# An output projection whose contraction drops from 4 row tiles to 3.5, with two heads sent into spare rows by DMA and the work after it moved in the issue order

## The chip, the cores and the metric

One core of a Trainium2 chip runs the whole kernel. Times are device microseconds (us). The trace is of one profiled execution of the same program. Engines: PE is the matrix engine (PEld its weight loads), ACT, DVE and POOL are the scalar, vector and general engines, and SP is the engine whose queue issues nearly all the DMAs of this kernel.

## The reference

Two transformer layers over x of shape [1, 2048, 448]: attention with 16 query heads of 28 columns and a single key and value head, then a gated feed-forward block. Both layers use the same weights.

```
q = (x @ wq) in 16 heads of 28;  k = x @ wk;  v = x @ wv
p = softmax(q . k / sqrt(28));   o = p @ v, the 16 heads side by side: 448 columns
attention(x) = o @ wo                               # the output projection
ffn(x)       = (silu(x @ w_gate) * (x @ w_up)) @ w_down
x = x + attention(layernorm(x));  x = x + ffn(layernorm(x))      # twice
```

## The kernel before, in words

The order of instructions on each engine is the order in which the code is written (manual scheduling): every engine works down its own list and waits on semaphores. What the change touches lies in the attention stage, `Attention.scores` (L600), run once in each layer.

**Work items.** The 2048 queries are four chunks c of 512 (NC = 4), the 16 heads four groups g of four (NG = 4). An item i = 4c + g is one group of heads on one chunk; i runs from 0 to 15. For each item the 16 key tiles kt are gone through (NT = 16), so the loop counter is n = 16 i + kt, and two key tiles make a double step d = n // 2. All three-term products use a value split into a rounded part and its remainder ("h" and "l" tiles).

**One step** (`step`, L630): 12 matmuls (L639), four heads at once in four strips of 32 rows of PE, write the scores of three heads into a `three` of three PSUM banks and of the fourth into a single bank (`one`, bank 6 or 7). ACT takes the exponentials: L651 (single bank) and L652 (`three`) in even steps, L646 (`three`) and L649 in odd ones, where DVE first copies the single bank out (L648, `raw`). After both steps of a double step, `pv` (L673) multiplies the probabilities of the double step before by the values (L680, 16 matmuls) into a single bank, and DVE adds that to the item's accumulator (L690, or L687 for the first).

**The end of an item** (`post` and `rest`, L694 to L722). Row 28 of each strip of 32 holds a head's denominators. They go by DMA to a small tile `rs` (L701). Three double steps later, at kt = 4 of the following item, DVE takes bounds and the reciprocal (L707 to L709), two DMAs spread the result through DRAM over the rows (`rd` L711, `o<-rd` L712), and POOL multiplies (L719) and splits into `onh`, `onl` (`split`, L139 and L140).

**The output projection** (`outproj`, L617). When the four items of chunk 0, 1 or 2 are done, the projection of that chunk is issued in `between` (L655) at kt = 10 of item 4c + 4: 4 row tiles of queries, each 4 groups x 3 terms = 12 matmuls of 128 rows x 448 columns, into two banks of `three`, then `one`, then the other single bank; each tile is followed by a DVE addition into the residual `xres` (L626). In a group's 128 rows only 4 x 28 carry heads; the rows of `wo` in between are set to zero (`load_wo`, L609, in items 2 and 3 at kt = 8). Chunk 3 is projected behind the loop.

**The layer norm of the finished chunk** is spread over key tiles by a table `later` (L726 to L738), from n = 16 (4c + 5) on: four statistics (DVE L240, L241), at offset 4 `scale` (POOL L246, L247: the reciprocal standard deviation `rstd`), from offset 5 on `apply` (DVE L255, reads `rstd`) and `turn` (DVE L260) by turns, then a DMA.

**Also on POOL:** at kt = 0 the split of the next item's queries (`parts`, L445), and at kt = 8 of items 11, 12 and 13 `weights` (L754): loads of the first feed-forward weights and 12 casts on POOL.

Of the kernel before, what the change touches and what calls it, by code (L numbers as in the profile page):

```python
# [9 lines left out]
F32R = mybir.dt.float32r  # L10
AF = mybir.ActivationFunctionType
ALU = mybir.AluOpType
# [3 lines left out]
P = 128  # L16
S = 2048
D = 448
H = 16
DH = 28  # L20
F = 1792
EPS = 1e-5
NT = S // P
NC = S // 512
NG = H // 4
# [27 lines left out]
def forward(  # L53
# [14 lines left out]
    nc = tc.nc  # L68
# [7 lines left out]
    wos = wo.rearrange("(g j d) n -> j d g n", g=NG, j=4)  # L76
# [46 lines left out]
    def dma(dst, src):  # L123
        nc.sync.dma_start(dst.bitcast(F32), src.bitcast(F32))
# [13 lines left out]
    def split(hi, lo, raw):  # L138
        nc.gpsimd.tensor_scalar(hi, raw, 1.0, 0.0, ALU.mult, ALU.add)  # L139
        nc.gpsimd.tensor_tensor(lo, raw, hi, ALU.subtract)  # L140

    xres = pers.tile([P, NT, D], F32, name="xres")
# [27 lines left out]
    def weights(fc):  # L170
        tiles, steps = parted(*loaded(fc))
        for f in steps:
            f()
        return tiles
# [178 lines left out]
    def side_by_side(lower, upper):  # L353

        assert len(lower) == len(upper)
        for two in zip(lower, upper):
            for po, (a, b), start, stop in two:
                nc.tensor.matmul(po, a, b, start=start, stop=stop, skip_group_check=True)  # L358
# [10 lines left out]
    class Attention:  # L369
# [230 lines left out]
        def scores(self, ff):  # L600
            next(switch)
            with tc.tile_pool(name=f"at{self.layer}", bufs=1, reuse_waits="tile") as wp:
                woh = wp.tile([P, NG, D], F32R, name="woh")
                wol = wp.tile([P, NG, D], F32R, name="wol")
                on, accs, pts = {}, {}, {}
                todo, due = [], {}
                single = lambda d: banks[6 + d % 2]

                def load_wo(z):  # L609
                    r = wpool.tile([P, 4, 2, P], F32, name="wr").rearrange("p (z k) b n -> p z (k b n)", z=2)  # L610
                    nc.gpsimd.memset(r, 0.0)
                    for j in range(4):
                        nc.sync.dma_start(r[32 * j : 32 * j + DH, :, 0:D], wos[j][:, 2 * z : 2 * z + 2, :])
                    zs = slice(2 * z, 2 * z + 2)
                    split(woh[:, zs, :], wol[:, zs, :], r[:, :, 0:D])

                def outproj(c, t, po, gs=range(NG)):  # L617
                    oh, ol = on[c]
                    ts_ = slice(P * t, P * t + P)
                    for g in gs:  # L620
                        for z, (a, b) in enumerate(((oh, woh), (oh, wol), (ol, woh))):
                            nc.tensor.matmul(  # L622
                                po[:, 0:D], a[:, g, ts_], b[:, g, :], start=(g + z == 0), stop=(g == NG - 1 and z == 2)
                            )
                    if gs[-1] == NG - 1:
                        return lambda: nc.vector.tensor_tensor(  # L626
                            xres[:, 4 * c + t, :], po[:, 0:D], xres[:, 4 * c + t, :], ALU.add
                        )
# [26 lines left out]
                def between(d):  # L655

                    i, kt = divmod(2 * d, NT)
                    free, one = threes[0], single(d + 1)
                    if full:
                        self.lent = free[:, 0, :]  # L660
                        if 6 <= kt < 14:
                            self.advance(min(NM // 4, NM * (i + 2) - self.done))
                        if kt == 14 and i + 1 < len(GR):
                            self.places[i + 1](free[:, 1, :])
                    if not todo or kt != 10:
                        return
                    c = todo.pop()
                    for f in [outproj(c, t, free[:, t, :]) for t in range(2)]:
                        f()
                    outproj(c, 2, one)()  # L670
                    outproj(c, 3, single(d))()

                def pv(d):  # L673

# [19 lines left out]
                def post(i):  # L694

                    c, g = GR[i]
                    out2 = accs.pop(i)
                    oraw, rb = out2[:, 0, :], out2[:, 1, :]
                    rs = wp.tile([P, 16], F32, name="rs", bufs=2)
                    for j in range(4):  # L700
                        nc.sync.dma_start(rs[32 * j : 32 * j + 32, :], oraw[32 * j + DH : 32 * j + DH + 1, :])  # L701

                    def rest():
                        if fine is not None:
                            under = wp.tile([P, 16], F32, name="under", bufs=2)
                            for bound, op in ((LIMIT, ALU.is_lt), (1.0 / LIMIT, ALU.is_gt)):
                                nc.vector.tensor_scalar(under, rs, bound, None, op)  # L707
                                nc.vector.tensor_tensor(fine, fine, under, ALU.mult)
                        nc.vector.reciprocal(rs, rs)  # L709
                        rd = dram.tile([4, 512], F32, name="rd", bufs=2)  # L710
                        nc.sync.dma_start(rd.rearrange("j (p n) -> (j p) n", n=16), rs)  # L711
                        nc.sync.dma_start(rb, rd[:, None, :].to_broadcast([4, 32, 512]))  # L712
                        if g == 0:
                            on[c] = (
                                wp.tile([P, NG, 512], F32R, name="onh"),
                                wp.tile([P, NG, 512], F32R, name="onl"),
                            )
                        oh, ol = on[c]
                        nc.gpsimd.tensor_tensor(rb, oraw, rb, ALU.mult)  # L719
                        split(oh[:, g, :], ol[:, g, :], rb)  # L720
                        if g == NG - 1 and c < NC - 1:
                            todo.append(c)  # L722

                    return rest

                later = {}  # L726
                for c in range(3):
                    ff.X[c] = xtile(xpool) if c < 2 else None
                    fs, got = norm_steps(c, lambda: pers.tile([P, 512], F32, name="sg"))
                    n = NT * (4 * c + 5)  # L730
                    for kt, f in enumerate(fs):
                        later[n + kt] = f
                    later[n + 22] = got["load"]
                    for k in range(4) if c < 2 else ():
                        for z in range(2):
                            later[n + 34 + 2 * k + z] = lambda c=c, got=got, k=k, z=z: flipped(
                                ff.X[c], k, got["raw"][:, k, :], nc.vector.tensor_copy, (z,)
                            )  # L738
                ff.norms[2] = got
                last = NT * len(GR)  # L740
                for n in range(last):
                    i, kt = divmod(n, NT)
                    if kt == 0 and i + 1 < len(GR):
                        self.parts(i + 1)
                    if kt == 3 and i + 1 < len(GR) and not full:
                        self.rows(i + 1)
                    if kt == 12 and i + 2 < len(GR):
                        self.stack(i + 2)
                    if i in (2, 3) and kt == 8:
                        load_wo(i - 2)  # L750
                    if n == NT and ff.nxt:
                        ff.nxt.below(nc.sync)
                    if kt == 8 and 10 < i <= 11 + FG:
                        ff.W[i - 11] = weights(i - 11)  # L754
                    step(n)
# [17 lines left out]
                pos = [bank(LOW)[1] for _ in range(4)]  # L773
# [10 lines left out]
    HALVES = slice(0, 64), slice(64, 128)  # L784
# [494 lines left out]
    for c in range(1, NC):  # L1279
        fs, got = norm_steps(c, n=2)  # L1280
        n = 4 * c - 4 - (c == 3)
# [40 lines left out]
```

## Time and profile before

| quantity | value |
|---|---|
| median of 3 runs | 1958.35 us (1958.0 to 1959.81) |
| the profiled execution | 1959.78 us, its trace spans 1958.0 us |
| PE clock granted in it | 0.999 |
| busy share of the span | PE 99%, PEld 67%, ACT 68%, DVE 52%, POOL 40% |
| DMA | 79.69 MB, 41 GB/s on average |

The span is what lies between the first and the last instruction; 1.8 us of the execution's time lie around it. A PE matmul's end is modelled, so "PE 99%" is not a PE at its peak: matmuls whose shown times overlap are counted over and over, and a PE that waits briefly shows hardly any gap. What bounds a stage is read from who waits for whom.

### The profile page before, as it was taken

Reading aid. Unit: us, or ns where it says so; the run is one execution under the profiler, and the core shown is the slowest. Engines: PE = TensorE matmul, PEld = TensorE weight load, DVE = VectorE, ACT = ScalarE, POOL = GpSimd, SP = SyncE. Lnnn points to the kernel's source line nnn. Section 1 sums busy time; section 2 is a strip of 40 time slices with the busy share of each in tenths; the row PEclk is TensorE's granted clock in tenths of the full one; section 3 lists DMA queues with packets and bytes.
Section 4 is the critical chain, followed back from the end, with each engine's and each line's share of the span. In section 5 each row is a group of like instructions: output and inputs, shape, how many; then the busy total and the mean of one; then the engine's idle time right before and its main releaser. Section 6 shows DMA issues by size and latency. Waiting matters only on the chain. (4 is left out here: it accounts for less than half of the span.)

```text
span 1958.0 us, 45644 instructions
## 1 busy us (share of the span) xinstructions
PE 1946.5 (99%) x18307; PEld 1312.0 (67%) x18307; DVE 1016.5 (52%) x1711; ACT 1338.3 (68%) x2353; POOL 774.2 (40%) x997
## 2 busy tenths in 40 slices
PE   9999999999999999999999999999999999999998
PEld 8544545445458899999984444454454688999997
DVE  7444543544425567665654335445454346666653
ACT  4899797998963344444349998979979533444432
POOL 5212111132314868766441221111232167688640
PEclk9999999999999999999999999999999999999999
DMA  5110020121210110111131011102121101110002
GB/s 167 54 30 26 23 49 22 31 59 28 73 33 2 53 32 21 28 32 27 52 114 33 27 31 31 45 12 62 30 53 48 33 7 48 33 32 22 27 17 77
DMA packets 100017, 79.69 MB, mean 41 GB/s; under 512 B 26040, under 2 KB 83000, under 8 KB 99800
## 3 DMA queue, kind: packets, MB, share of 16 engines
q1 hardware_dynamic: 99224, 75.81, 14.2%
q8 instruction: 144, 2.36, 0.5%
q10 hardware_dynamic: 576, 0.92, 0.1%
q14 instruction: 73, 0.60, 0.1%
HBM read 57.15 MB, written 18.74 MB: 39 GB/s over the span
## 5 line engine op out<-in xcount | busy, mean ns | idle before, releaser
L680 PE MATMUL bank<-pt,vsb 128*32 128x512 f32 x4096 | 493.3, 598 | 0.3
L639 PE MATMUL bank<-qstack,keys 32*128 32x512 f32 x1536 | 484.5, 425 | 0.0
L639 PE MATMUL three<-qstack,keys 32*128 32x512 f32 x4608 | 460.2, 425 | 1.5 <-DVE vt L573 1.2
L639 PEld LDWEIGHTS three<-qstack,keys 32*128 32x128 f32 x4608 | 254.0, 182 | 295.4 <-ACT pt L652 178.6
L646 ACT ACTIVATE pt<-three 128x1536 f32<-128x1536 f32 x256 | 372.2, 1454 | 1.2 <-PE bank L680 0.8
L652 ACT ACTIVATE pt<-three 128x1536 f32<-128x1536 f32 x256 | 372.0, 1453 | 0.0
L358 PE MATMUL bank<-xh,wgh 64*128 64x512 f32 x1344 | 355.0, 392 | 0.3 <-DVE sg L1119 0.3
L358 PE MATMUL bank<-wdh,h 64*128 64x448 f32 x1776 | 324.3, 364 | 0.1
L648 DVE COPY raw<-bank 128x512 f32<-128x512 f32 x256 | 177.1, 692 | 226.8 <-PE bank L639 223.9
L358 PE MATMUL bank<-xh,wgl 64*128 64x512 f32 x1020 | 286.2, 390 | 0.0
L690 DVE TENSOR_TENSOR o<-bank,o 128x512 f32<-128x512 f32 x224 | 154.9, 692 | 240.5 <-PE bank L680 235.6
L719 POOL TENSOR_TENSOR o<-o 128x512 f32<-128x512 f32 x32 | 41.3, 1290 | 593.5 <-DMA o<-rd 462.1
L680 PEld LDWEIGHTS bank<-pt,vsb 128*32 128x32 f32 x4096 | 107.1, 109 | 249.9 <-issue 153.3
L365 ACT COPY seen<-bank 128x1 f32<-128x1 f32 x788 | 99.3, 163 | 244.4 <-PE bank L358 183.7
L358 PE MATMUL bank<-xl,wgh 64*128 64x512 f32 x912 | 247.9, 390 | 0.0
L639 PEld LDWEIGHTS bank<-qstack,keys 32*128 32x128 f32 x1536 | 243.3, 183 | 1.3 <-DVE o L690 0.6
L358 PEld LDWEIGHTS bank<-wdh,h 64*128 64x128 f32 x1776 | 225.9, 184 | 11.0 <-issue 2.0
L358 PE MATMUL bank<-wdl,h 64*128 64x448 f32 x888 | 204.7, 366 | 0.0
L358 PEld LDWEIGHTS bank<-xh,wgh 64*128 64x128 f32 x1344 | 191.5, 184 | 13.5 <-issue 0.9
L905 POOL TENSOR_TENSOR xres<-stage,xres 128x448 f32<-128x448 f32 x120 | 152.1, 1280 | 112.0 <-ACT stage L898 111.8
L651 ACT ACTIVATE pt<-bank 128x512 f32<-128x512 f32 x256 | 151.4, 592 | 60.8 <-PE bank L639 60.6
L870 DVE TENSOR_TENSOR xn<-bank,xn 128x512 f32<-128x512 f32 x192 | 126.5, 687 | 124.9 <-PE bank L358 94.2
(205 smaller groups left out, 3064.4 us busy)
## 6 DMA issues: line engine op xcount, KB each, us to landing
o<-rd SPq DMA_DIRECT2D x32, 256.0 KB
qraw<-qd SPq DMA_DIRECT2D x128, 56.0 KB
qd<-stage SPq DMA_DIRECT2D x30, 224.0 KB
xt<-xn SPq DMA_DIRECT2D x28, 224.0 KB
wdr<-in_B_w_down_dram SPq DMA_DIRECT2D x28, 224.0 KB
wr<-in_B_w_gate_dram SPq DMA_DIRECT2D x32, 192.0 KB
wr<-in_B_w_up_dram SPq DMA_DIRECT2D x32, 192.0 KB
xn<-xt SPq DMA_DIRECT2D x6, 768.0 KB
```

The source lines that it names most:

```text
L358: nc.tensor.matmul(po, a, b, start=start, stop=stop, skip_group_check=True)
L365: nc.scalar.copy(seen[:, i : i + 1], po[:, 0:1])
L639: nc.tensor.matmul(three[:, j, :] if j < 3 else one, k[js, kp, ks], q[js, part, :], start=(z == 0), stop=(z == 2), tile_position=(32 * j, 0),)
L646: nc.scalar.activation(pt, three, AF.Exp, scale=SCALE)
L648: nc.vector.tensor_copy(raw, one)
L651: nc.scalar.activation(pt1, one, AF.Exp, scale=SCALE)
L652: nc.scalar.activation(pt, three, AF.Exp, scale=SCALE)
L680: nc.tensor.matmul(po[32 * j : 32 * j + 32, :], vsb[:, n % NT, :], pts[n][j], start=(n == 2 * d), stop=(n > 2 * d), skip_group_check=True,)
L690: nc.vector.tensor_tensor(acc, in_turn(po), acc, ALU.add)
L719: nc.gpsimd.tensor_tensor(rb, oraw, rb, ALU.mult)
L870: plus = lambda out, po, r: tt(by_tile(out), in_turn(po), by_tile(r), ALU.add)
L905: nc.gpsimd.tensor_tensor(r, h[e, t], r, ALU.add)
```

## The change

**Heads 14 and 15 go into spare rows.** `load_wo` gets a second form, "dense", for chunks 0 to 2: the 56 rows of `wo` of these two heads are loaded four at a time into the four spare rows (28 to 31) of 14 strips, and those of heads 12 and 13 are loaded twice, in rows 0 to 63 and 64 to 127 of group 3. The zeroing on POOL is dropped in that form. `onh` and `onl` become one tile `on`, and `spread` moves the normalised rows of heads 14 and 15 in the same way: 14 DMAs of 4 rows x 4 KB and one of 64 rows x 4 KB on SP's queue, issued at the end of `rest` for the last item of a chunk, for 3 chunks in each layer.

**The projection** (`dense`) then has, for each tile, 3 groups x 3 terms = 9 matmuls of 128 rows and 3 of 64 rows; the 64-row matmuls of two tiles are issued as pairs in the two halves of PE's rows. Tiles go in two twos, and the DVE additions follow each two. Chunk 3 keeps `outproj`, with `wo` loaded again in the zeroed form in item 14 at kt = 0 and kt = 8.

**The places in the order.** The projection moves from kt = 10 of item 4c + 4 to kt = 2 of item 4c + 5. The whole `later` table of a chunk starts 4 key tiles (two double steps) later: statistics at kt = 4 to 7 of item 4c + 5, `scale` at kt = 8, `apply` at kt = 9, 11, 13 and 15. The casts of `wo` are no longer issued behind their loads but put into `later` by halves, 5 to 7 key tiles on.

The rows below are the engines' lists as issued. POOL in item 5 of the first layer (chunk 0): `o` is the accumulator of item 4, `rstd` belongs to chunk 0's norm. Before:

```order
L140 TENSOR_TENSOR qstack_100<-qraw,qstack_100 128x512
L246 TENSOR_SCALAR rstd<-mv 128x4
L247 TENSOR_TENSOR rstd<-rstd,halfn 128x4
L719 TENSOR_TENSOR o_2399<-o_2399 128x512
L139 TENSOR_SCALAR onh<-o_2399 128x512
L140 TENSOR_TENSOR onl<-o_2399,onh 128x512
```

The same place now:

```order
L140 TENSOR_TENSOR qstack_100<-qraw,qstack_100 128x512
L752 TENSOR_TENSOR o_2412<-o_2412 128x512
L139 TENSOR_SCALAR on<-o_2412 128x512
L140 TENSOR_TENSOR on<-o_2412,on 128x512
L246 TENSOR_SCALAR rstd<-mv 128x4
L247 TENSOR_TENSOR rstd<-rstd,halfn 128x4
```

The two `rstd` instructions stood ahead of the three that finish an item; now they stand behind them. POOL in item 13 (chunk 2), where the casts of `weights(2)` (`wgh`, `wgl`, `wdh`, `wdl`) are issued too, now:

```order
L752 TENSOR_TENSOR o_5607<-o_5607 128x512
L139 TENSOR_SCALAR on<-o_5607 128x512
L140 TENSOR_TENSOR on<-o_5607,on 128x512
L139 TENSOR_SCALAR wgh<-wr 128x256
...
L140 TENSOR_TENSOR wdl<-wdr,wdh 128x224
L246 TENSOR_SCALAR rstd<-mv 128x4
L247 TENSOR_TENSOR rstd<-rstd,halfn 128x4
L139 TENSOR_SCALAR qstack_101<-qraw 128x512
```

There `rstd` stood ahead of the first of these rows; now the three instructions of the item and all 12 casts (ten of them left out here) come first. DVE in item 13 around the first `apply` (L255) now; `raw` is the copy that ACT waits for, `o2` the accumulator:

```order
L726 TENSOR_TENSOR o2_6016<-bank7_79,o2_6016 128x512
L686 COPY raw_6236<-bank7_79 128x512
L255 TENSOR_SCALAR sg_6240<-xres_89,mv_91,rstd_6218 128x448
L726 TENSOR_TENSOR o2_6016<-bank6_78,o2_6016 128x512
L260 STREAM_TRANSPOSE xn_6239<-sg_6240 128x448
L686 COPY raw_6283<-bank6_78 128x512
```

Behind the `apply` stand the addition that frees bank 6 and the next copy out of it. The order around an `apply` is as before; what moved is that this first one stands at kt = 9, where the third one stood. PE at the end of the projection of chunk 0 now (`bank_78` is bank 6, `bank_79` bank 7; L358 are the 64-row matmuls, L677 the next step's scores):

```order
L358 MATMUL bank_78<-woh,on 128x448
L358 MATMUL bank_79<-woh,on 128x448
L358 MATMUL bank_78<-wol,on 128x448
L358 MATMUL bank_79<-wol,on 128x448
L358 MATMUL bank_78<-woh,on 128x448
L358 MATMUL bank_79<-woh,on 128x448
L677 MATMUL three_808<-qstack_101,keys_96 128x512 x3
L677 MATMUL bank_78<-qstack_101,keys_96 128x512
```

Both banks get their last matmul at the very end, and the fourth matmul of the next step writes bank 6 again; before, twelve matmuls into the other bank stood between the last into bank 6 and that one. The diff:

```
-                def load_wo(z):
+                def load_wo(z, dense):
                     r = wpool.tile([P, 4, 2, P], F32, name="wr").rearrange("p (z k) b n -> p z (k b n)", z=2)
-                    nc.gpsimd.memset(r, 0.0)
+                    if not dense:
+                        nc.gpsimd.memset(r, 0.0)
+                    spare = wo[14 * DH : 16 * DH, :].rearrange("(q r) n -> r q n", r=4)
                     for j in range(4):
-                        nc.sync.dma_start(r[32 * j : 32 * j + DH, :, 0:D], wos[j][:, 2 * z : 2 * z + 2, :])
-                    zs = slice(2 * z, 2 * z + 2)
-                    split(woh[:, zs, :], wol[:, zs, :], r[:, :, 0:D])
+                        for up in (0, 64) if dense and z and j < 2 else (0,):
+                            own = slice(2 * z + bool(up), 2 * z + (1 if dense and z and j > 1 else 2))
+                            to = slice(bool(up), own.stop - 2 * z)
+                            p0 = up + 32 * j
+                            nc.sync.dma_start(r[p0 : p0 + DH, to, 0:D], wos[j][:, own, :])
+                            if dense:
+                                qs = slice(4 * own.start + j, 4 * own.stop - 3 + j, 4)
+                                nc.sync.dma_start(r[p0 + DH : p0 + 32, to, 0:D], spare[:, qs, :])
+
+                    def cast(a):
+                        split(woh[:, 2 * z + a, :], wol[:, 2 * z + a, :], r[:, a, 0:D])
+
+                    return [lambda: cast(0), lambda: cast(1)]
+
+                def spread(o):
+                    for q in range(14):
+                        p0 = 64 + 4 * q + 4 * (q > 6)
+                        dma(o[32 * (q % 4) + DH : 32 * (q % 4) + 32, q // 4], o[p0 : p0 + 4, 3])
+                    dma(o[64:128, 3], o[0:64, 3])
+
+                def dense(c, ts, pos):
+                    o = on[c]
+                    cols = [slice(P * t, P * t + P) for t in ts]
+                    terms = ((0, woh), (0, wol), (1, woh))
+                    for cs, po in zip(cols, pos):
+                        for g in range(3):
+                            for z, (v, b) in enumerate(terms):
+                                nc.tensor.matmul(
+                                    po[:, 0:D], o[:, g, v, cs], b[:, g, :], start=(g + z == 0), stop=False, skip_group_check=True
+                                )
+                    side_by_side(
+                        *(
+                            [(po[:, 0:D], (o[rs, 3, v, cs], b[rs, 3, :]), False, z == 2) for z, (v, b) in enumerate(terms)]
+                            for cs, po, rs in zip(cols, pos, HALVES)
+                        )
+                    )
+                    for t, po in zip(ts, pos):
+                        x = xres[:, 4 * c + t, :]
+                        nc.vector.tensor_tensor(x, po[:, 0:D], x, ALU.add)
...
-                    if not todo or kt != 10:
+                    if not todo or kt != 2:
                         return
                     c = todo.pop()
-                    for f in [outproj(c, t, free[:, t, :]) for t in range(2)]:
-                        f()
-                    outproj(c, 2, one)()
-                    outproj(c, 3, single(d))()
+                    dense(c, (0, 1), (free[:, 0, :], free[:, 1, :]))
+                    dense(c, (2, 3), (one, single(d)))
...
                         nc.gpsimd.tensor_tensor(rb, oraw, rb, ALU.mult)
-                        split(oh[:, g, :], ol[:, g, :], rb)
+                        split(o[:, g, 0, :], o[:, g, 1, :], rb)
                         if g == NG - 1 and c < NC - 1:
+                            spread(o)
                             todo.append(c)
...
-                    n = NT * (4 * c + 5)
+                    n = NT * (4 * c + 5) + 4
                     for kt, f in enumerate(fs):
                         later[n + kt] = f
...
                     if i in (2, 3) and kt == 8:
-                        load_wo(i - 2)
+                        later[n + 5], later[n + 7] = load_wo(i - 2, True)
+                    if i == 14 and kt in (0, 8):
+                        later[n + 6], later[n + 7] = load_wo(kt // 8, False)
```

More of the change, by code (lines that the diff above doesn't have):

```diff
@@ L617, in outproj @@
                 def outproj(c, t, po, gs=range(NG)):
-                    oh, ol = on[c]
+                    oh, ol = (on[c][:, :, v, :] for v in range(2))
                     ts_ = slice(P * t, P * t + P)
@@ L713, in rest @@
                         if g == 0:
[L714 to L718, printed above, removed]
+                            on[c] = wp.tile([P, NG, 2, 512], F32R, name="on")
+                        o = on[c]
                         nc.gpsimd.tensor_tensor(rb, oraw, rb, ALU.mult)
-                        split(oh[:, g, :], ol[:, g, :], rb)
+                        split(o[:, g, 0, :], o[:, g, 1, :], rb)
                         if g == NG - 1 and c < NC - 1:
+                            spread(o)
                             todo.append(c)
```

## The prediction, made before the changed kernel ran

> **What bounds the kernel now.** I read the page first: its span, and ACT's share by slice.
>
> ```profile
> span 1958.0 us, 45644 instructions
> ACT  4899797998963344444349998979979533444432
> ```
>
> PE shows 99% everywhere, but ACT shows a different picture in slices 2 to 11 and 22 to 31, the two attention stages: it is nearly full there and a third full elsewhere. So I asked who waits for whom. First the score matmuls' line (L639), its waits and their count:
>
> ```profile
> its engine sat idle before it (us, times) until:
>   ACT pt L652: 178.6, 213
>   ACT pt L646: 73.2, 248
> ```
>
> then ACT's first exponential of an even step (L651):
>
> ```profile
>   PE bank L639: 60.6, 8
> ```
>
> PE's weight loads wait 252 us for ACT in 461 places; ACT waits for PE 60.6 us in only 8. **In attention ACT is the bound, and PE follows it.** The eight are the two starts and six projections. At the first projection (chunk 0, first layer):
>
> ```profile
> 200.39 1.28 POOL L140 TENSOR_TENSOR onl<-o,onh 128x512 fp32r<-128x512 f32 x1
> ...
> 200.86 0.47 PE L622 MATMUL three<-woh,onh 128*128 128x448 f32 x1
> ...
> 201.54 0.62 ACT L649 ACTIVATE pt<-raw 128x512 f32<-128x512 f32 x1
> ...
> 208.20 0.37 PE L622 MATMUL bank<-woh,onl 128*128 128x448 f32 x1
> ...
> 210.68 0.37 PE L622 MATMUL bank<-woh,onl 128*128 128x448 f32 x1
> 210.97 0.50 PE L639 MATMUL three<-qstack,keys 32*128 32x512 f32 x3
> 210.99 0.49 PE L639 MATMUL bank<-qstack,keys 32*128 32x512 f32 x1
> ...
> 211.08 0.62 DVE L626 TENSOR_TENSOR xres<-bank,xres 128x448 f32<-128x448 f32 x1 [1.85 <-PE bank L622]
> ...
> 212.05 0.60 ACT L651 ACTIVATE pt<-bank 128x512 f32<-128x512 f32 x1 [9.89 <-PE bank L639]
> ...
> 215.74 0.59 ACT L651 ACTIVATE pt<-bank 128x512 f32<-128x512 f32 x1
> ```
>
> ACT has run dry while PE projects and stands 9.89 us; the next double step, bound by ACT, takes 3.69 (212.05 to 215.74). What counts in these stages is ACT's idle time: what shortens a projection is gained in full, and what keeps scores from ACT is lost in full. I price the change by that.
>
> **The projection itself.** From the twelfth matmul before the end (208.20) to the last (210.68) are 12 steps: 0.207 us for a matmul of 128 x 448. The row-paired matmuls of the feed-forward stage, same width:
>
> ```profile
> 704.95 0.41 PE L358 MATMUL bank<-wdh,h 64*128 64x448 f32 x2
> 705.15 0.41 PE L358 MATMUL bank<-wdl,h 64*128 64x448 f32 x2
> ```
>
> A pair takes 0.20 us, as much as one full matmul. So 48 slots become 36 + 6 = 42: 6 x 0.207 = **1.24 us less** for each of six projections. Against it: the step from the last projection matmul to the scores, where the row tiling changes, took 0.29 instead of 0.207; three more such changes cost 3 x 0.085 = 0.25. And a new wait: both banks now finish together, and the fourth score matmul writes bank 6 again. Before, the addition out of a bank started 0.40 us after its last matmul's start (210.68, 211.08) and took 0.62, so bank 6 comes free 1.02 us after; the score matmul stood 0.31 after it (210.99). It comes 0.7 late, with the wake-up some 0.8 (estimate). Net 1.24 - 0.25 - 0.8 = 0.2 less; **six: 1.2 us less**. Ends: 7.4 less, if neither charge holds, and about 2 more, if each costs half as much again.
>
> **The norm steps, two double steps later.** This is where I put the large term. Everything in POOL's list waits behind what stands ahead. `scale` (`rstd`) now stands behind the end of an item, whose multiplication waits for a DMA. Item 5, first layer, before:
>
> ```profile
> 225.48 0.20 POOL L246 TENSOR_SCALAR rstd<-mv 128x4 f32<-128x4 f32 x1 [7.18 <-DVE mv L241]
> 225.77 1.02 POOL L247 TENSOR_TENSOR rstd<-rstd,halfn 128x4 f32<-128x4 f32 x1
> ...
> 228.29 0.50 DVE L255 TENSOR_SCALAR sg<-xres,mv,rstd 128x448 f32<-128x448 f32 x1
> ...
> 232.93 0.57 SPq L712 DMA_DIRECT2D o<-rd  x1
> ...
> 236.03 0.51 DVE L255 TENSOR_SCALAR sg<-xres,mv,rstd 128x448 f32<-128x448 f32 x1
> ...
> 238.47 1.29 POOL L719 TENSOR_TENSOR o<-o 128x512 f32<-128x512 f32 x1 [11.69 <-DMA o<-rd]
> ```
>
> `rstd` was ready at 226.8, 1.5 us ahead of the first `apply`. The projection now comes ahead of kt = 4 in the same total time, so from kt = 4 on this clock still holds within a microsecond. The first `apply` now stands where the third stood, at 236.03. `rstd` now has to wait for the multiplication that starts at 238.47, when the broadcast issued at 232.93 has landed, and then for it, the split and itself. Without a clash these last, by the second layer's rows:
>
> ```profile
> 1207.84 1.30 POOL L719 TENSOR_TENSOR o<-o 128x512 f32<-128x512 f32 x1 [11.09 <-DMA o<-rd]
> ...
> 1209.93 1.30 POOL L140 TENSOR_TENSOR onl<-o,onh 128x512 fp32r<-128x512 f32 x1
> ```
>
> 3.4 us from 1207.84 to 1211.23, and 1.3 for the two `rstd` instructions (225.48 to 226.79): 4.7 together. So DVE stands at the `apply` for 238.47 + 4.7 - 236.03 = 7.1 us, and behind it stand the addition that frees a score bank and ACT's next copy. In the same way, from the third `apply` and the multiplication of the other two cases of this kind:
>
> ```profile
> 364.46 0.51 DVE L255 TENSOR_SCALAR sg<-xres,mv,rstd 128x448 f32<-128x448 f32 x1
> 1205.63 0.50 DVE L255 TENSOR_SCALAR sg<-xres,mv,rstd 128x448 f32<-128x448 f32 x1
> 1333.86 0.51 DVE L255 TENSOR_SCALAR sg<-xres,mv,rstd 128x448 f32<-128x448 f32 x1
> ```
> ```profile
> 368.64 1.29 POOL L719 TENSOR_TENSOR o<-o 128x512 f32<-128x512 f32 x1 [13.07 <-DMA o<-rd]
> 1336.08 1.29 POOL L719 TENSOR_TENSOR o<-o 128x512 f32<-128x512 f32 x1 [11.12 <-DMA o<-rd]
> ```
>
> 8.9, 6.9 and 6.9 us. For chunk 2, in item 13, the 12 casts of `weights(2)` come in between as well:
>
> ```profile
> 492.54 0.50 DVE L255 TENSOR_SCALAR sg<-xres,mv,rstd 128x448 f32<-128x448 f32 x1
> 495.66 1.29 POOL L719 TENSOR_TENSOR o<-o 128x512 f32<-128x512 f32 x1 [12.02 <-DMA o<-rd]
> ...
> 499.02 0.41 POOL L139 TENSOR_SCALAR wgh<-wr 128x256 fp32r<-128x256 f32 x1
> ...
> 506.01 0.61 POOL L139 TENSOR_SCALAR qstack<-qraw 128x512 fp32r<-128x512 f32 x1
> ```
> ```profile
> 1463.14 0.50 DVE L255 TENSOR_SCALAR sg<-xres,mv,rstd 128x448 f32<-128x448 f32 x1
> 1466.04 1.28 POOL L719 TENSOR_TENSOR o<-o 128x512 f32<-128x512 f32 x1 [11.78 <-DMA o<-rd]
> ```
>
> Those take 506.01 - 499.02 = 7.0 us: DVE stands 3.1 + 4.7 + 7.0 = 14.8 us here and 14.6 in the second layer. The six make 59.2 us.
>
> ACT has a cushion: what PE has already scored. When DVE stops, at 236.03, ACT still takes the odd step's copy and the whole next even step, whose bank is free; it wants the following `three` at:
>
> ```profile
> 240.12 1.46 ACT L646 ACTIVATE pt<-three 128x1536 f32<-128x1536 f32 x1
> ```
>
> 4.1 us later. Those scores stand still, because their fourth matmul writes the bank that DVE's addition has not freed. Once `rstd` is there, the `apply` (0.5), the addition (0.6) and the rest of the step's matmuls (from a step's fourth matmul at 210.99 to ACT at 212.05: about 1.1, and a wake-up) take 2.3 us until ACT runs. ACT loses the stand less 4.1 plus 2.3, that is less 1.8: 59.2 - 6 x 1.8 = **48.4 us more**. ACT is the bound, so nothing later makes up for it. Both ends of this term: nothing, if the cushion covered all, and 59.2.
>
> The Trainium skill, "Perfetto Trace Analysis", section "Tensor Engine Instruction (MATMUL, LD_WEIGHTS)", says that ACT, DVE and GPSIMD are strict FIFO, while PE may pull weight loads ahead. That speaks against this change: by it nothing behind a waiting `rstd` or `apply` can pass, and the term stays at 48; without it, the sum would end at the 1.2 us gained. No row of before shows DVE held up at an `apply`, so the page cannot be tested by them.
>
> **The rest I cost at nothing.** `spread`: SP can start when the split ends (`onl`, 201.7). It is hidden by the four double steps by which the projection comes later: first matmul at 200.86 + 4 x 3.69 = 215.6, the pairs, behind 18 matmuls, at 219.3. The nearest issues of like DMAs, a copy within the on-chip memory and the four `rs`:
>
> ```profile
> L124 SPq DMA_DIRECT2D xd<-xh x4: 527/568/596, 576.9 to 1548.1; - x4
> ```
> ```profile
> 440.34 2.47 SPq L701 DMA_DIRECT2D rs<-o  x4
> ```
>
> By both an issue takes about 0.6: 15 make 9. The last copy waits for the fourteen before it (estimate 2), and needs at most the 5.5 us of the 256 KB broadcast (232.93 to 238.47): about 218. The cover is thin; where it goes, each microsecond is lost six times. SP's later issues (query loads, `rs`, `rd`) have double steps to spare. POOL's new casts in item 14 lie behind that item's end, where nothing on DVE reads from POOL before item 15; SP's queue waits there for POOL's zeroing, and nothing in it is due until then.
>
> **Sum.** 1959.8 + 48.4 - 1.2 = 2007 us for the profiled execution, which stood 1.4 above the median: **2006 us**, 2.4% slower.
>
> **Rivals.**
> *Not slower: a waiting instruction is passed.* The 48 us rest on POOL and DVE keeping their lists. If POOL ran the ready `rstd` ahead of the multiplication that waits for its DMA, it would be there as early as before, ahead of kt = 9, and only the projection would count: 1957 us, and 1952 if the bank wait did not come about either (six times 1.0 less instead of 0.2). The point from which it decides is a stand of 1.8 us; below it ACT notices nothing. Against it: in all six places the multiplication starts 2.2 to 4.2 us behind the third `apply`, and `rstd` is written behind it.
> *Only chunk 2 pays.* If `o<-rd` lands 5.3 us sooner, now that SP's queue has other DMAs before it, the stands of chunks 0 and 1 fall below 1.8 us. In chunk 2 the casts still stand in between: 9.5 and 9.3 us of stand are left, of which ACT loses 7.7 and 7.5: 15.2 - 1.2 = 14 more, 1972 us. For it: the one landing of chunk 1 in the first layer came 2 us later than its like, so landings move. Against: 5.3 of the 5.5 us would have to go.
> *`spread` is late.* If SP took its 15 DMAs one landing after the other, at an estimated 2 us each, the last would land 30 us after the split, 12 behind the pairs' turn: six times that on top, 2078. Against: the four `rs` issues of the row above follow at 0.6 us each, with no landing between them.
>
> **Chances.** Forecast 0.80; only chunk 2 pays 0.07; not slower at 1957 0.05, at 1952 0.03; `spread` late 0.05. A measurement of this kernel can tell about 0.2% (3.9 us) from no change. Faster 0.03, same 0.05, slower 0.92. The range leaves the rivals out (0.20) and takes in the forecast's own bounds: down to 1981, if each landing comes 2 us sooner (as chunk 1's varied) and ACT restarts at once (2.3 us), six times 4.3 less; up to 2023, with the whole 59.2 lost and a microsecond lost at each `spread` (six each of 1.8 and 1.0).
>
> **What would show it.** Right: DVE's waits in the new profile name POOL `rstd` at an `apply`, four times about 7 and twice about 15 us; ACT has six new gaps of 5 to 13 us in items 5, 9 and 13; the six projection gaps stay near 9.7. Wrong: `rstd` ahead of 236 on this clock, no such gaps, or PE waiting for DMAs at the first projection matmul.

## The result and the profile after

| | before | after |
|---|---|---|
| median (6 runs each) | 1958.18 us (1957.71 to 1959.81) | 2028.81 us (2028.02 to 2031.59) |
| profiled execution, span | 1959.78, 1958.0 us | 2031.39, 2029.5 us |
| PE clock granted in it | 0.999 | 0.983 |
| each attention stage | 508 and 509 us | 543 and 543 us |
| feed-forward between them | 461 us | 461 us |

The changed kernel takes 1.0362 times as long, interval 1.0349 to 1.0375: 70.6 us more. The forecast was 47.8 more, and its range ended at 2023. So the direction held and the size did not.

The page of the changed kernel, ACT's busy tenths and PE's clock by slice:

```profile
span 2029.5 us, 45898 instructions
...
ACT  4899699698683344444349996988977633444442
...
PEclk9999999899899999999999998999998999999999
```

ACT falls to 6 in slices 5, 8 and 11 of the first attention stage, and to 6 and 7 in slices 25, 30 and 31 in the second. PE's clock has eights in slices 8, 11, 25 and 31; before it had none. Next, the waits of ACT and of DVE (total, times, longest):

```profile
ACT pt L684 <- PE bank L716: 65.4, 9, 16.4
ACT pt L689 <- DVE stats L240: 59.1, 6, 9.9
ACT pt L689 <- PE bank L677: 5.1, 7, 1.2
...
DVE sg L255 <- POOL rstd L247: 59.9, 6, 15.7
```

The last row is the stand that the prediction priced at 59.2 us: DVE at the first `apply` of a chunk, waiting for POOL's `rstd`, six times, 59.9 us. The second row is the six projections: 59.1 us against 60.0 before. The first row is new. Its count of 9 holds six long gaps (7.71, 9.08 and 15.04 us in the first layer; 7.85, 7.92 and 16.40 in the second, 64.0 together) and three short ones. With the third row these make the loss. (DVE's `stats` is named as releaser in the second row only because it finished last by the profile; the exponential waits for PE's scores.)

Chunk 0 of the first layer in order of time, selected rows of POOL, DVE, PE and ACT (start, duration, then idle time before and releaser):

```profile
238.19 1.26 POOL L752 TENSOR_TENSOR o<-o 128x512 f32<-128x512 f32 x1 [19.26 <-DMA o<-rd]
...
239.54 0.62 POOL L139 TENSOR_SCALAR on<-o 128x512 fp32r<-128x512 f32 x1
240.24 1.26 POOL L140 TENSOR_TENSOR on<-o,on 128x512 fp32r<-128x512 f32 x1
241.58 0.20 POOL L246 TENSOR_SCALAR rstd<-mv 128x4 f32<-128x4 f32 x1
241.87 1.01 POOL L247 TENSOR_TENSOR rstd<-rstd,halfn 128x4 f32<-128x4 f32 x1
242.91 0.51 DVE L255 TENSOR_SCALAR sg<-xres,mv,rstd 128x448 f32<-128x448 f32 x1 [7.04 <-POOL rstd L247]
243.34 0.68 DVE L726 TENSOR_TENSOR o<-bank,o 128x512 f32<-128x512 f32 x1
...
244.07 0.79 PE L677 MATMUL bank<-qstack,keys 32*128 32x512 f32 x1 [5.89 <-DVE o L726]
...
245.64 2.87 PE L716 MATMUL bank<-pt,vsb 128*32 128x512 f32 x16
...
247.69 1.45 ACT L684 ACTIVATE pt<-three 128x1536 f32<-128x1536 f32 x1 [7.71 <-PE bank L716]
```

This is the cascade, each row released by the one above: `rstd` behind the end of the item, `apply` behind `rstd`, the addition that frees a bank behind `apply`, the scores behind the addition, and ACT behind the scores and the value matmuls (L716), which by its row ended last. DVE began to stand at 242.91 - 7.04 = 235.87; ACT ran dry at 247.69 - 7.71 = 239.98. So the cushion was 4.1 us, as forecast. But from `apply` to ACT it took 247.69 - 242.91 = **4.78 us, where the forecast had 2.3**. The other five cases, read in the same way, give the same: a cushion of 4.1 and a restart r of 4.78 or 4.79 us each, so 64.0 = 59.9 - 6 x 4.1 + 6 x 4.78.

PE's clock in four stretches around it (columns: us, then busy time and instructions of PE, PEld, DVE, ACT, POOL, then PE's granted clock, DMA share, GB/s):

```profile
228.00:238.00 10.00, 10.00 (x111) 4.10 (x103) 5.89 (x16) 10.00 (x11) 0.00 (x0) 1.00 0.23 52
...
239.00:240.70 1.70, 0.00 (x0) 0.00 (x0) 0.00 (x0) 0.97 (x1) 1.53 (x3) 1.00 0.00 0
240.90:247.50 6.60, 3.43 (x21) 1.38 (x25) 3.12 (x5) 0.00 (x0) 1.80 (x3) 0.50 0.00 1
247.70:252.00 4.30, 4.30 (x48) 1.60 (x40) 2.71 (x4) 4.30 (x5) 0.00 (x0) 1.00 0.00 0
```

PE stands idle for 5.89 us, from 238.18 to 244.07. The clock is halved by 240.9, after 2.7 us of that, and is full again in the stretch from 247.7, 3.6 us after the restart. The 16 value matmuls at 245.64 take 2.87 us at the low clock. The Trainium skill, "TensorE: Matmul & The Clock Gate", section "What's actually happening", says that about 3.4 us without work drop PE to half its clock and that it needs as long again busy to get it back. The trace agrees with the half clock (0.50) and nearly with the time back (3.6 us). The idle time that it took was shorter than the page's, 2.7 us here, and 1.71 and 3.06 us in experiments 7 and 8; there the measurement decides. The prediction had not used the rule.

The first projection, at its end and at the start of its copies:

```profile
201.62 11.10 SPq L124 DMA_DIRECT2D on<-on  x15
...
225.12 0.51 PE L677 MATMUL three<-qstack,keys 32*128 32x512 f32 x3
...
225.91 0.49 PE L677 MATMUL bank<-qstack,keys 32*128 32x512 f32 x1 [0.28 <-DVE xres L653]
...
226.95 0.60 ACT L689 ACTIVATE pt<-bank 128x512 f32<-128x512 f32 x1 [9.86 <-DVE stats L240]
```

The fourth score matmul stands 0.79 us behind the first, for the bank: the forecast's 0.8. The gap is 9.86 us where 9.89 stood. PE waits for no DMA there.

### The profile page after: what moved, and what is told of

It is laid out like the page before. It is cut to its first block, busy times and chain, and to the rows that moved or that the text cites. A ratio compares the mean times of both kernels' runs of the same rounds, so it can differ in the third digit from the quotient of the medians.

```text
span 2029.5 us, 45898 instructions
## 1 busy us (share of the span) xinstructions
PE 1960.7 (97%) x18307; PEld 1319.0 (65%) x18307; DVE 1021.4 (50%) x1711; ACT 1339.8 (66%) x2353; POOL 789.9 (39%) x1021
## 4 chain that ended last, share of the span: by engine, by line
PE 45%; DMA 2%; POOL 1%; DVE 1%; issue 1%; ACT 0%; SPq 0%; DVEq 0%; POOLq 0%; ACTq 0%
PE bank L358 19%; PE bank L716 11%; PE three L677 8%; PE bank L677 2%; PE bank L338 2%; DMA o<-rd 1%; PE bank L642 1%; PE three L642 1%; DMA rd<-rs 0%; PE bank L304 0%; POOL o L752 0%; POOL on L140 0%; DMA qraw<-qd 0%; PE bank L461 0%; POOL rstd L247 0%
## 5 line engine op out<-in xcount | busy, mean ns | idle before, releaser
L677 PE MATMUL bank<-qstack,keys 32*128 32x512 f32 x1536 | 489.1, 428 | 55.3 <-DVE o L726 53.6
L716 PE MATMUL bank<-pt,vsb 128*32 128x512 f32 x4096 | 502.6, 608 | 0.7
L677 PE MATMUL three<-qstack,keys 32*128 32x512 f32 x4608 | 467.5, 428 | 1.5 <-DVE vt L573 1.2
L677 PEld LDWEIGHTS three<-qstack,keys 32*128 32x128 f32 x4608 | 257.9, 185 | 297.0 <-ACT pt L690 169.3
L358 PE MATMUL bank<-xh,wgh 64*128 64x512 f32 x1344 | 367.8, 392 | 0.3 <-DVE sg L1155 0.3
L358 PE MATMUL bank<-wdh,h 64*128 64x448 f32 x1776 | 328.9, 364 | 0.1
L358 PE MATMUL bank<-xh,wgl 64*128 64x512 f32 x1020 | 294.4, 390 | 0.0
L677 PEld LDWEIGHTS bank<-qstack,keys 32*128 32x128 f32 x1536 | 247.5, 185 | 61.9 <-DVE o L726 56.4
L716 PEld LDWEIGHTS bank<-pt,vsb 128*32 128x32 f32 x4096 | 108.3, 110 | 255.9 <-issue 161.4
L358 PE MATMUL bank<-xl,wgh 64*128 64x512 f32 x912 | 257.4, 390 | 0.0
L358 PEld LDWEIGHTS bank<-wdh,h 64*128 64x128 f32 x1776 | 235.9, 184 | 8.2 <-issue 2.0
L358 PE MATMUL bank<-wdl,h 64*128 64x448 f32 x888 | 212.0, 366 | 0.0
L358 PEld LDWEIGHTS bank<-xh,wgh 64*128 64x128 f32 x1344 | 201.9, 185 | 11.2 <-issue 0.9
L689 ACT ACTIVATE pt<-bank 128x512 f32<-128x512 f32 x256 | 151.0, 590 | 64.4 <-DVE stats L240 59.1
```

Source lines behind the costliest of these rows:

```text
L677: nc.tensor.matmul(three[:, j, :] if j < 3 else one, k[js, kp, ks], q[js, part, :], start=(z == 0), stop=(z == 2), tile_position=(32 * j, 0),)
L689: nc.scalar.activation(pt1, one, AF.Exp, scale=SCALE)
L716: nc.tensor.matmul(po[32 * j : 32 * j + 32, :], vsb[:, n % NT, :], pts[n][j], start=(n == 2 * d), stop=(n > 2 * d), skip_group_check=True,)
```

## The experiments

Each ratio is to the kernel before, run beside that experiment; its median there was 1958.8 to 1959.2 us.

**1. The shift of the norm alone**, in the kernel before:

```
-                    n = NT * (4 * c + 5)
+                    n = NT * (4 * c + 5) + 4
```

> The kernel before with one line changed: the norm table of each chunk starts 4 key tiles later, the projection stays as it was and where it was. Theory A (the norm shift alone makes the loss: rstd stands behind an item's end on POOL, DVE stands at the first apply, ACT starves): DVE stands about 7 us at four applies and about 15 us at two, six new ACT gaps of 7.5 to 16.5 us, and about 2028 us, 70 us above before. Theory B (the new projection, its spread DMAs or the later place carry part of the loss): clearly less, 2006 us if the norm term has the size that was predicted for it.

Measured: 2028.86 us, ratio 1.0356 (1.034 to 1.0372), clock 0.984. Waits of this kernel (here L651 is the exponential of the single bank, with the projections; L646 that of a `three`):

```profile
ACT pt L651 <- PE bank L639: 64.8, 13, 10.2
ACT pt L646 <- PE bank L680: 64.2, 8, 16.7
...
DVE sg L255 <- POOL rstd L247: 59.5, 6, 16.0
```

One number in one line makes the whole loss: the same stands, the same gaps, the same lower clock. What else the change does (dense weights, copies, pairs, projection one item later) comes to nothing in sum within the intervals.

**2. The casts of item 13 two key tiles later**, so that they are issued behind `rstd`:

```
-                    if kt == 8 and 10 < i <= 11 + FG:
+                    if kt == (10 if i == 13 else 8) and 10 < i <= 11 + FG:
```

> The changed kernel, but the weight casts of item 13 are issued at kt = 10, behind rstd, instead of kt = 8. Theory A (POOL's list order holds rstd back): the stand at chunk 2's first apply falls by the 7.1 us of the casts, from 14.4 and 15.7 us to 7.3 and 8.6; about 14 us less in all, 2014 us. Theory B (rstd and the casts wait for the same DMA traffic, or POOL passes waiting work): stands as before, 2029 us.

Measured: 2017.19 us, ratio 1.0294 (1.0278 to 1.031), 11.6 us less than the changed kernel.

```profile
ACT pt L684 <- PE bank L716: 52.9, 10, 9.8
...
DVE sg L255 <- POOL rstd L247: 46.5, 6, 9.0
```

DVE's stands are 13.4 us shorter (59.9 to 46.5) and none is longer than 9.0: the casts were the second half of the two long ones, as the prediction had it.

**3. The end of the item behind `rstd` as well**: the multiplication and split of the first item after a projected chunk are issued at kt = 8, behind `scale`; with the edit of experiment 2.

```
+                        if g or not c:
+                            finish()
+                        else:
+                            due[8 * i + 12] = finish
+
+                    def finish():
...
```

> The changed kernel with POOL's order mended: for the item whose end falls into the norm (the first of chunks 1 to 3) POOL's multiplication and split are issued at kt = 8 behind rstd, their DMAs stay at kt = 4; the casts of item 13 go to kt = 10. Theory A: no DVE stand at an apply, no ACT gap but the six projections of about 9.85 us, 1957 to 1958 us. Theory B (something else in the change costs too: spread, the wo loads, the place at kt = 2): what is left above 1960 us.

Measured: 1963.76 us (1960.33 to 1967.03), ratio 1.0024 (1.0014 to 1.0034). In its profile (of an execution of 1960.96 us) there is no stand at `rstd` ahead of an `apply` any more and PE's clock is 0.999. **So POOL's order is the cause of 65 of the 70.6 us.** The 1957 to 1958 expected did not come. What the profile shows to be left stands in item 14, where DVE waits for the denominators, 5.0 us in two places by the waits:

```profile
DVE under L743 <- DMA rs<-o: 5.0, 2, 3.1
```

The second layer's place in order of time, SP's queue, DVE and ACT:

```profile
1479.93 1.64 SPq L619 DMA_DIRECT2D wr<-in_A_wo_dram  x4
1481.67 3.57 SPq L269 DMA_DIRECT2D xt<-xn  x4
1485.34 3.27 SPq L737 DMA_DIRECT2D rs<-o  x4
...
1489.88 0.17 DVE L743 TENSOR_SCALAR under<-rs 128x16 f32<-128x16 f32 x1 [3.09 <-DMA rs<-o]
...
1491.48 0.63 ACT L687 ACTIVATE pt<-raw 128x512 f32<-128x512 f32 x1 [1.11 <-DVE raw L686]
```

The loads of `wo` wait at the head of SP's queue for POOL's zeroing, the stores of the finished chunk (`xt`, shifted with the norm) come next, and the `rs` copies, which DVE waits for, are third. ACT loses only 1.9 us by these waits in this execution, one of the quickest of the nine; of the longer ones there is no profile.

**4. That queue mended too**: the loads of `wo` in item 14 and the store of a chunk two key tiles later, behind the `rs` copies.

```
-                        later[n + kt] = f
+                        later[n + kt + 2 * (kt == len(fs) - 1)] = f
...
-                    if i == 14 and kt in (0, 8):
+                    if i == 14 and kt in (2, 10):
```

> order_fixed with two groups of DMAs moved behind the item's small rs loads on SP's queue: the zeroed wo load of item 14 goes from kt = 0 and 8 to kt = 2 and 10, the norm's store to DRAM two key tiles later. Theory A (in order_fixed those loads and the store stood ahead of rs in SP's queue, and DVE stood 1.9 and 3.1 us at the bounds, which read rs): these stands go, only the six projection gaps are left, 1957 to 1958 us and a spread of runs like that of before. Theory B (order_fixed's 1960 to 1967 comes from elsewhere, such as landings that vary): as order_fixed, 1963 us.

Measured: 1958.12 us, ratio 0.9995 (0.9986 to 1.0005), with no wait for `rs` left, and a spread of runs (1957.58 to 1959.48) like that of before. That is 5.6 us less than experiment 3: the second cost of the change. Which of the two groups of DMAs makes it was not separated. In the changed kernel itself it lay hidden beneath the larger cost: the same three groups stand in the same order there (1545.65, 1547.38 and 1550.54), but POOL had been idle for 12.27 us ahead of its zeroing, and DVE waits nowhere for `rs`. What remains after both is no difference from the kernel before.

**5 and 6. The bank wait taken out.** On top of experiment 4, the 64-row pairs of the last two row tiles are issued ahead of their full matmuls, so that bank 6 gets its last matmul nine earlier and its addition is done when the scores come:

```
+                    early = ts[0] == 2
...
+                    if early:
+                        pairs()
...
```

> queue_fixed with the 64-row pairs of row tiles 2 and 3 issued ahead of their full matmuls instead of behind them, so that tile 2 is complete nine matmuls (1.9 us) before tile 3. Theory A (the fourth score matmul waits 0.5 to 0.8 us for the addition out of bank 6, and one change of row tiling less is needed): each of six projection gaps falls from 9.85 to about 9.0, 5 us less than queue_fixed, 1952 to 1953 us. Theory B (ACT does not wait for that bank): at most the tiling change, 0.1 us each, 1957 us.

Measured: **1952.15 us, ratio 0.9966 (0.9954 to 0.9978)**, faster than both kernels, by 0.34% against the one before. With the pairs first in both halves (`early = True`), where the copies of `spread` are needed 18 matmuls, 3.7 us, sooner:

> As queue_fixed_pairs_first, but the pairs of row tiles 0 and 1 come first too, so that the projection starts with the rows that the last spread copy writes, 3.7 us earlier than in the changed kernel. It measures how late spread lands. Theory A (SP ends its 15 issues about 11 us after the split, the last copy lands some 3 us later, at the time of the first projection matmul): PE waits 0 to 2 us at the first pair in each chunk, 1950 to 1963 us, not better than queue_fixed_pairs_first. Theory B (spread lands with microseconds to spare): no wait, one tiling change less, 1952 us. Theory C (spread lands much later than its issue): more than 1970 us.

Measured: 1953.17 us, ratio 0.997 (0.9958 to 0.9982). ACT's wait for scores, in the first of the two kernels and then in the second (six projections and two stage starts in one row):

```profile
ACT pt L701 <- PE bank L689: 54.1, 8, 8.9
```
```profile
ACT pt L701 <- PE bank L689: 55.1, 8, 9.1
```

In the first, ACT's gap at a projection is about 1 us shorter than in experiment 4 (at most 8.9, where it was 9.9). The 1.0 that the prediction gave for a projection without the bank wait came. In the second, PE waits for no DMA at a projection, so the copies would have been in time even 3.7 us sooner; why its gaps are about 0.2 longer each is not shown.

**7. PE kept busy**: in the changed kernel, 26 throw-away matmuls (60 in item 13) into a free `three`, ahead of the first scores that stand. This adds work whose results nothing reads; it leaves POOL's order alone.

```
+                    if i in (5, 9, 13) and kt == 11:
+                        for _ in range(60 if i == 13 else 26):
+                            nc.tensor.matmul(
+                                threes[n % 2][:, 0, 0:D], keys[0][:, 0, 0:P], qts[i % 2][:, 0, 0:D],
+                                start=True, stop=True, skip_group_check=True,
+                            )
```

> The changed kernel with extra matmuls, whose results are thrown away, ahead of the score matmuls of kt = 11 in items 5, 9 (26 each, 5.4 us) and 13 (60, 12.4 us), where PE would stand idle; nothing of the stand itself is taken away. Theory A (PE's granted clock, 0.5 to 0.6 behind the stand, makes the restart slow): the clock stays at 1.0, scores and values run at full pace, the first ACT gap of each stand is 1.6 us shorter and the second one mostly gone, 10 to 14 us less in all, 2015 to 2019 us. Theory B (the restart is long because ACT's probability buffer is freed only behind the value matmuls, whatever the clock): 2029 us or above.

Measured: 2014.72 us, ratio 1.0282 (1.0266 to 1.0298), clock 0.998. The same place in order of time, and then the stretch behind it with its clock:

```profile
237.65 5.48 PE L793 MATMUL three<-qstack,keys 128*128 128x448 f32 x26
...
244.80 1.92 PE L716 MATMUL bank<-pt,vsb 128*32 128x512 f32 x16
...
245.97 1.45 ACT L684 ACTIVATE pt<-three 128x1536 f32<-128x1536 f32 x1 [6.10 <-PE bank L716]
```
```profile
244.00:248.00 4.00, 4.00 (x45) 1.83 (x49) 3.00 (x5) 2.03 (x3) 0.00 (x0) 1.00 0.00 0
```

The clock stays at 1.00 here, the 16 value matmuls take 1.92 us instead of 2.87, and ACT's gap is 6.10 instead of 7.71. From `apply` to ACT it takes 3.23 us in five of the six stands. In the sixth (chunk 2, second layer) it takes 4.26, and there the clock still fell, after only 1.71 us without a matmul:

```profile
1518.31 0.50 PE L677 MATMUL bank<-qstack,keys 32*128 32x512 f32 x1 [1.71 <-DVE o L726]
```
```profile
1519.00:1522.30 3.30, 3.30 (x21) 0.59 (x16) 1.24 (x3) 0.90 (x1) 0.00 (x0) 0.50 0.00 0
```

A kernel with 112 more matmuls a layer is 14 us quicker than without them. So **the clock after PE's idle time is about 14 of the 70.6 us**. But the six long gaps still sum to 53.6 with stands of 57.8: r = (53.6 - 57.8 + 24.6) / 6 = 3.4 us, not yet 2.3.

**8 and 9. The value matmuls ahead of the scores that stand.** ACT's exponential behind the stand writes a probability buffer `pt`, of which there are three; the value matmuls that must read it first were issued behind the scores that stand. Here `pv` goes ahead of them:

```
+                    moved = i in (5, 9, 13) and kt in (10, 11)
+                    if moved and not odd:
+                        pv(d - 1)
...
-                        if d:
+                        if d and not moved:
```

> The changed kernel, but in items 5, 9 and 13 the value matmuls of key tiles 8 and 9 are issued ahead of the score matmuls of kt = 11, on which PE stands, instead of behind them; they are ready and can run while DVE stands. Theory A (a part of the slow restart is ACT's wait for its probability buffer, which these matmuls free): the first ACT gap of each stand falls by about 2 us, the second one goes, 13 to 16 us less in all, 2013 to 2016 us, with the clock still low behind the stand. Theory B (only the clock matters): 2029 us, less at most the matmuls' own 1.9 us of one place, 2027 us.

Measured: 2025.67 us, ratio 1.0338 (1.0321 to 1.0356): 3 us, where 13 to 16 were expected. Waits and clock of this kernel:

```profile
ACT pt L684 <- PE three L677: 49.8, 6, 14.5
ACT pt L684 <- PE bank L716: 8.9, 11, 1.2
ACT pt L689 <- PE bank L677: 6.7, 11, 0.9
```
```profile
241.30:244.30 3.00, 0.00 (x0) 0.00 (x0) 1.16 (x3) 0.00 (x0) 1.64 (x3) 1.00 0.01 3
244.40:245.00 0.60, 0.60 (x12) 0.40 (x12) 0.60 (x2) 0.00 (x0) 0.00 (x0) 1.00 0.00 0
245.10:251.80 6.70, 5.76 (x41) 2.44 (x37) 3.69 (x7) 4.51 (x5) 0.00 (x0) 0.50 0.00 0
251.90:256.00 4.10, 4.10 (x48) 1.60 (x40) 3.23 (x4) 3.85 (x5) 1.81 (x2) 1.00 0.00 0
```

The buffer wait is real: the first gaps shrink by 14.2 (64.0 to 49.8, r = 2.3). But PE's clock still falls, here after only 3.06 us without work and 0.7 us behind the restart, and PE is then too slow to feed ACT: 9.1 of the 14.2 come back as second and third gaps (the last two rows of waits, 15.6 together, where the changed kernel has 6.5). With both, 15 and 49 throw-away matmuls and `pv` ahead:

> Both: the value matmuls of key tiles 8 and 9 ahead, and extra matmuls with thrown-away results (15 in items 5 and 9, 49 in item 13) behind them, up to shortly before the stand ends. Theory A (low clock and buffer wait together make up the restart beyond what was predicted): the first ACT gaps come near the stand less 1.8 us, 5.2, 6.6, 12.6, 5.4, 5.4 and 13.9 us, the second ones are gone; 2029 less some 20, 2007 to 2011 us. Theory B (something else holds ACT back): not below pe_kept_busy, 2014 us.

Measured: 2012.38 us, ratio 1.0275 (1.0258 to 1.0292), clock 0.998. Chunk 0 again, PE, DVE, ACT:

```profile
240.21 3.34 PE L793 MATMUL three<-qstack,keys 128*128 128x448 f32 x15
...
242.41 0.51 DVE L255 TENSOR_SCALAR sg<-xres,mv,rstd 128x448 f32<-128x448 f32 x1 [6.88 <-POOL rstd L247]
...
244.55 1.45 ACT L684 ACTIVATE pt<-three 128x1536 f32<-128x1536 f32 x1 [4.91 <-PE bank L677]
```

From `apply` to ACT: 244.55 - 242.41 = 2.14 us, and 2.0 to 2.3 in all six. The six first gaps are 45.6 with stands of 57.7, that is the stand less 2.0. With the clock kept and the buffer free, the prediction's term (the stand less 1.8) is what is seen. Further short gaps of 5.4 us remain, and the time missed the 2007 to 2011 expected by a little. Against the busy PE alone the first gaps are 8.0 us shorter and the short ones 1.9 longer, but the median is only 2.3 us lower (4.3 between the two profiled executions). So what the buffer wait costs by itself is known only as 2 to 6 us, and most of the 14 us by which the first gaps shrank in experiment 8 was delay that PE's low clock handed on to the gaps behind.

A fourth probability buffer, the plainest test of the buffer wait, is not among the runs.

## Why the prediction missed

The direction, the six stands and their cause came as forecast; the price of a stand did not, and ACT's six gaps were 7.7 to 16.4 us where 5 to 13 were forecast.

**The projection: right in that it comes to little.** Forecast 1.2 us less in six, measured 0.8 less (59.97 to 59.13). But that lies in one gap, which before was 10.90 us; the other five together are 0.2 longer, so 0.2 less at each was not seen. The bank wait was 0.79, and experiment 5 shows what it hid.

**DVE's stands: right.** 59.2 forecast, 59.9 measured, each stand within 1.2 us of its forecast, and by the cause named: the end of the item (experiment 3) and the casts (experiment 2). The order of POOL and DVE held strictly: by the Trainium skill's rule on strict FIFO ("Perfetto Trace Analysis", section "Tensor Engine Instruction (MATMUL, LD_WEIGHTS)"), nothing behind a waiting instruction passes it, and the six stands of 7 to 16 us now bear that out.

**ACT's loss from a stand: the step that failed.** The prediction said that "the rest of the step's matmuls (...) take 2.3 us until ACT runs". It took the 1.1 us from a step's fourth matmul to ACT from a place where PE was at full clock and no buffer was short, and the sum has no term for the clock. Measured: 4.78 us, six times 2.5 more, 14.9 us; with 0.7 of longer stands that is the whole difference between 48.4 and 64.0. Two things stand in that place: PE's clock falls while it stands idle (experiment 7), and ACT's next exponential needs a buffer whose readers stand in PE's list behind the blocked scores (experiments 8 and 9). With the clock kept alone, r is 3.4; with the buffer freed alone it is 2.3, but later gaps grow; with both it is 2.1, near the 2.3 of the prediction.

**"ACT is the bound, so nothing later makes up for it": true, but it gets worse.** Behind five of the six stands there is a second gap of 0.5 to 1.3 us a double step later; with one more of 0.8 they sum to 5.2 us. They were not in the forecast. With PE kept busy one second gap of 0.4 is left, behind the stand where the clock still fell, so they belong to the clock as well; the 0.8 stays, and its cause is open.

The sum against the forecast for the profiled execution, 2007: 15.6 (first gaps) + 5.2 (later gaps) + 0.4 (projection) = 21.2 of the 24.4 missing. Most of the other 3 us lies behind the attention stages: from the last exponential to the end this execution took 424.5 us, the one of before 422.0 and experiment 1's 422.1. That execution stood 2.6 above its median.

**Costed at nothing.** The copies of `spread`: right (issued in 11.1 us where 9 were estimated, and early enough even in experiment 6). SP's queue in item 14, of which it was said that "nothing in it is due until then": wrong, since `rs` was due and 5.6 us appear once the larger stand is gone (experiments 3 and 4). It did not show in the time of the changed kernel.

**The rivals.** None came about. The first, a waiting instruction that is passed, gave 1957 and 1952 as the worth of the projection without the stand, the second of them without the bank wait too. Experiments 4 and 5 measured 1958.12 and 1952.15. The second has a slip: with a landing 5.3 us sooner the stand of 8.9 would still be 3.6, above the 1.8 from which ACT loses.

## What to carry to other kernels

When work is moved in an issue order by hand, walk each engine's list past it: a small instruction that lands behind one that waits for a DMA stops its own engine, and then each engine that reads from it. Price such a stand as its length less the cushion plus the restart, and do not take the restart from a place in full flow: here the matmuls behind a stand ran at half the clock, and a buffer whose readers stood behind the blocked instruction was short as well (4.78 us, where 2.3 had been read). Where a large loss is found, mend it and measure again, since smaller ones lie beneath it (here 5.6 us in a queue, and 6 us of gain in the order of two matmul groups).

## What the runs showed of the hardware

- In the changed kernel PE's granted clock was halved during a stand of 5.89 us without work, by 2.7 us into it, and was full again 3.6 us after the restart. In chunk 2, after 13.21 us without work (to 526.13), it stayed at 0.50 for 4.8 us more:

```profile
517.40:530.80 13.40, 4.67 (x25) 1.43 (x25) 3.12 (x5) 1.05 (x1) 6.95 (x13) 0.50 0.00 0
531.00:535.00 4.00, 4.00 (x48) 1.77 (x48) 2.70 (x4) 3.51 (x5) 0.00 (x0) 1.00 0.00 0
```

- 3.06 us without work (experiment 8) were enough for it, and there the low clock came late, from 245.1 to 251.8, behind the restart at 244.31. Once 1.71 us were enough (experiment 7), for 3.3 us.
- Throw-away matmuls in the idle time kept it at 1.00 in five of six stands, and were worth 14 us of 2029.
- Fifteen copies within the on-chip memory were issued from one queue in 11.1 us, 0.74 each.
